# Attention and two feed-forward stages on one core: column norms issued behind the scores, w_out's conversion behind the second normed tile, and the softmax bias from a scaled pass with an accumulator

## The chip, the cores and the metric

The kernel runs on one core of one Trainium2 chip. The metric is the device time of one execution in microseconds (us), lower is better. Five engines work side by side, each through its own queue in order: TensorE (PE, its weight loads PEld), VectorE (DVE), ScalarE (ACT), GpSimd (POOL) and SyncE (SP), which issues the DMAs.

## What is computed

Cut to what matters, with B, H, S, D = 4, 8, 576, 64:

```python
scores = q @ k.T / sqrt(64)
thresh = scores.max(-1) - tau
attn = softmax(where(scores >= thresh, scores, -1e9)) @ v
x = attn as [2304, 512]
xn = x / rms(x) * rms_g
x = (silu(xn @ w_gate) * (xn @ w_val)) @ w_out      # widths 512, 1536
P = Sinkhorn(exp(x @ moe2_w_gate - max), 8 rounds)   # 8 experts
out = sum over e of P[:, e] * (relu(x @ w1[e]) @ w2[e])   # width 1024
```

Large products are made from pairs of f16 numbers (a high and a low part), so every operand is scaled, rounded and split first. The weights of the first feed-forward stage arrive as 64-bit words, from which VectorE and ScalarE build f32 by bit operations.

## The kernel before

The attention runs tile by tile: 144 tiles, a tile being 128 rows of one head (or two heads with 64 rows each). `att_tile` writes the scores S (128 x 576) to one of two PSUM buffers. VectorE takes the row maximum (L292), ScalarE turns it into the bias of the exponential (L293) and into the threshold (L297), and takes the exponential (L296). VectorE zeroes what is below the threshold and sums the rows (L298). ScalarE and GpSimd split the result in two f16 parts (L303 to L305), a DMA transposes it to eT (L307), and `att_values` multiplies it by v (L330). The pv matmuls of a tile are issued three tiles later, behind the scores of that tile (LAG = 3, `tc.issue_after`). `prepare` loads, scales and transposes q, k and v, for the next batch too (ks L225, qs L256, vs L242).

When the eight heads of 128 rows are done, `end_main` and `finish_x` divide by the sums, norm the rows (xn, L353) and transpose them to xnT. Two such tiles are one token group of the first feed-forward stage. `mlp_in` makes 12 blocks gv (L530, 24 matmuls each, both weights) and from each a u (L539, L540) and its parts tT; `mlp_out` multiplies by w_out into two x (L561, 36 matmuls each). There are nine groups. The first can only start when w_gate and w_val are converted (`prep_in`, called six times, by `prep_group`), and its x only when w_out is (`prep_out`).

`prep_in` loads four blocks of words, builds f32 (`to_f32`: L432 on ScalarE; L433, L435 and L436 on VectorE), squares them (L456), and TensorE sums the squares over the partitions into column norms (L457), from which the scale and the two f16 parts follow (L465, L466). The f32 values lie in three stages in the space that later holds w_out. `prep_out` does the like for 12 blocks of w_out with the same `to_f32`, one `words` buffer for the even blocks (x2) and one for the odd (x2t), takes one maximum (womxp, L131), and then scales each block (wof, L507), rounds it (L508) and splits off the rest (L509, GpSimd).

After the attention come the last groups and the second feed-forward stage (h L860, y L906), 16 half experts of dense matmuls.

The program text is not the order: a list scheduler puts each engine's instructions in order by priority at build time, attention first (`attention_order`), and the chip runs each queue as it stands. `tc.issue_after(ins)` puts what a block issues on the engine of `ins` behind `ins` in that engine's queue, and nothing else.

Of the kernel before, what the change touches and what calls it, by code (L numbers as in the profile page):

```python
# [7 lines left out]
F32 = mybir.dt.float32  # L8
F16 = mybir.dt.float16
BF16 = mybir.dt.bfloat16  # L10
I32 = mybir.dt.int32
AF = mybir.ActivationFunctionType
# [7 lines left out]
def kernel(  # L20
# [29 lines left out]
    P = 128  # L50
# [142 lines left out]
    def prep_q_scales(st):  # L193

        b, qr = st["b"], st["raw_q"]
        s_k, i_k = st["k"]
        qm = small([P, NW], "qm", bufs=2)
        for c in range(NW):
            sq = pa.tile([P, H, 2, D], F16, tag="ks", name=f"qq{b}_{c}", bufs=2)
            A.activation(  # L200
                sq[:, :, 0, :].bitcast(BF16), qr[:, :, c, :], AF.Square, accum_out=qm[:, c : c + 1]
            )
        s_q, i_q = norm_scale(qm, NW, 9, f"q{b}")

        wt = small([P, NW], f"wt_{b}")
        bt = small([P, NW], f"bt_{b}")
        V.tensor_scalar(bt, s_q, s_k[:, 0:1], ntau8[:, 0:1], ALU.mult, ALU.mult)
        c2 = small([P, NW], f"c2_{b}")
        V.tensor_scalar(c2, i_q, i_k[:, 0:1], z8[:, 0:1], ALU.mult, ALU.mult)
        V.tensor_scalar(wt, i_q, i_k[:, 0:1], nz8[:, 0:1], ALU.mult, ALU.mult)  # L210
        st.update(wt=wt, bt=bt, c2=c2, s_q=s_q)

    def prep_k(st, a):

# [51 lines left out]
    HS = S // 2  # L266

    waiting = []
    LAG = 3

    def att_tile(st, c, heads, slot, group):

        kT = st["kT"]
        qT, qX = st["q", c]
        nm = f"{st['b']}_{c}_{heads[0]}"
        sums = group["sums"]
        sp = psa.tile([P, 2, 512], F32, tag="S", name=f"S{nm}", bufs=2)
        rows = P // len(heads)
        for qq, first in ((qT, True), (qX, False)):
            for i, h in enumerate(heads):  # L280
                for j in range(2):
                    last = T.matmul(  # L282
                        sp[i * rows : (i + 1) * rows, j, 0:HS],
                        lhsT=qq[:, h, 0:rows],
                        rhs=kT[h // H2][:, h % H2, j * HS : (j + 1) * HS],
                        start=first,
                        stop=not first,
                    )
        sv = sp[:, :, 0:HS]
        nt = pa.tile([P, 3], F32, tag="nt", name=f"nt{nm}", bufs=4)  # L290
        mx = nt[:, 2:3]
        V.tensor_reduce(mx, sv, AX.XY, ALU.max)  # L292
        A.activation(nt[:, 0:1], mx, AF.Copy, scale=st["wt"][:, c : c + 1])  # L293
        e = pa.tile([P, S], F32, tag="e", name=f"e{nm}", bufs=3)
        ev = e.rearrange("p (a n) -> p a n", a=2)
        A.activation(ev, sv, AF.Exp, bias=nt[:, 0:1], scale=st["c2"][:, c : c + 1])  # L296
        A.activation(nt[:, 1:2], mx, AF.Identity, bias=st["bt"][:, c : c + 1])  # L297
        V.scalar_tensor_tensor(  # L298
            ev, sv, nt[:, 1:2], ev, ALU.is_ge, ALU.mult, accum_out=sums[:, slot : slot + 1]
        )  # L300

        hl = pa.tile([P, 2 * S], F16, tag="hl", name=f"hl{nm}", bufs=3)
        A.activation(hl[:, 0:S], e, AF.Copy)  # L303
        G.tensor_tensor(hl[:, S + REM :], e[:, 0 : NCH * P], hl[:, 0 : NCH * P], ALU.subtract)  # L304
        G.tensor_tensor(hl[:, S : S + REM], e[:, NCH * P :], hl[:, NCH * P : S], ALU.subtract)  # L305
        eT = pa.tile([P, 2 * S // P, P], F16, tag="eT", name=f"eT{nm}", bufs=3)
        nc.sync.dma_start_transpose(out=eT, in_=hl)  # L307
        waiting.append((st, heads, slot, group, eT))
        if len(waiting) > LAG:

            with tc.issue_after(last.ins):
                att_values(*waiting.pop(0))
# [25 lines left out]
        return rs  # L338

    xnT = {}  # L340

    def finish_x(i, x, ivx):

        ssq = pa.tile([P, 1], F32, tag="ssq", name=f"ssq{i}", bufs=2)
        xn = pa.tile([P, 2, DM], F16, tag="xn", name=f"xn{i}", bufs=1)
        A.activation(xn[:, 0, :].bitcast(BF16), x, AF.Square, scale=ivx, accum_out=ssq)
        ms = pa.tile([P, 1], F32, tag="ms", name=f"ms{i}", bufs=2)
        V.tensor_scalar(ms, ssq, 1.0 / DM, 1e-6, ALU.mult, ALU.add)
        rs = pa.tile([P, 1], F32, tag="rs", name=f"rs{i}", bufs=2)
        G.tensor_tensor(rs, ms, mhalf, ALU.pow)  # L350
        V.tensor_scalar(rs, rs, 16.0, ivx, ALU.mult, ALU.mult)
        A.activation(xn[:, 0, :], x, AF.Copy, scale=rs[:, 0:1])
        V.scalar_tensor_tensor(xn[:, 1, :], x, rs[:, 0:1], xn[:, 0, :], ALU.mult, ALU.subtract)  # L353
        j, o = i // 2, (i % 2) * P
        if o == 0:
            xnT[j] = pw.tile([P, 2 * KD, 2 * P], F16, tag="xnT", name=f"xnT{j}", bufs=2)
        nc.sync.dma_start_transpose(
            out=xnT[j][:, :, o : o + P], in_=xn.rearrange("p l d -> p (l d)")
        )
# [79 lines left out]
        return lw  # L439

    staged = [0]

    def prep_in(src, w, gi, name):

        bits = src.bitcast(I32)
        raw = stage[:, staged[0] % 3]
        staged[0] += 1
        ps = psm.tile([P, DM], F32, tag="mm", name=f"{name}n{gi}")
        cols = slice(gi * DM, (gi + 1) * DM)
        for kk in range(KD):  # L450
            wd = words(
                bits[kk * P : (kk + 1) * P, 2 * gi * DM : 2 * (gi + 1) * DM], f"{name}w{gi}_{kk}"
            )
            to_f32(raw[:, kk], wd, f"{name}l{gi}_{kk}")
            sq = pw.tile([P, 2 * P], F32, tag="u", name=f"{name}q{gi}_{kk}", bufs=2).bitcast(BF16)
            A.activation(sq, raw[:, kk], AF.Square)  # L456
            T.matmul(ps, lhsT=gsq[:, kk : kk + 1].to_broadcast([P, P]), rhs=sq, start=kk == 0, stop=kk == KD - 1)  # L457
        n2 = small([P, 1], name + "n2", bufs=2)
        V.tensor_reduce(n2, ps, AX.X, ALU.max)
        s, inv = norm_scale(n2, 1, 9, f"{name}{gi}")  # L460
        gs = small([P, KD], f"{name}gs{gi}")
        V.tensor_scalar(gs, g_sb, s[:, 0:1], None, ALU.mult)
        for kk in range(KD):
            sk, hi = gs[:, kk : kk + 1], w[:, 0, kk, cols]
            A.activation(hi, raw[:, kk], AF.Copy, scale=sk)  # L465
            V.scalar_tensor_tensor(w[:, 1, kk, cols], raw[:, kk], sk, hi, ALU.mult, ALU.subtract)  # L466
        return inv
# [14 lines left out]
    def prep_out():  # L482
# [3 lines left out]
        om = small([P, KF], "om")  # L486
        for f in range(KF):
            wd = words(bits[f * P : (f + 1) * P, :], f"wo{f}", ("x2", "x2t")[f % 2])
            sq = to_f32(wo32[:, f], wd, f"wol{f}").bitcast(BF16)[:, 0:DM]
            A.activation(sq, wo32[:, f], AF.Square, accum_out=om[:, f : f + 1])  # L490
        for _ in range(2):
            V.tensor_tensor(
# [488 lines left out]
```

## Time and profile before

| | us |
|---|---|
| median of 3 runs | 2197.92 (2195.69 to 2199.4) |
| profiled execution, its own time | 2195.02 |
| span of that execution, first to last instruction | 2193.2 |
| busy: PE / DVE / ACT / POOL | 2032.0 / 1490.2 / 870.9 / 471.0 |
| chain that ended last | PE 70% of the span |

A busy share is a mean over stages with different limits, so the stages are read one by one, by windows of the trace. A row of waits names who waited, for what, the sum in us, how often and the longest. A row of a group of instructions gives line, engine, operation, output and inputs, shapes, count, busy us, mean ns of one, and the idle time ahead of them with what ended it. Matmuls are pipelined, so the rows of matmuls overlap. Line numbers are those of the kernel before; in the changed kernel the same code stands some 5 to 20 lines further down.

### The profile page before, as it was taken

The numbers are of one execution on the slowest core, as the hardware profiler recorded it, in microseconds if no ns is written. First come the engines' busy times: TensorE is split into PE (matmuls) and PEld (weight loads), VectorE is DVE, ScalarE is ACT, GpSimd is POOL, SyncE is SP. The second block draws the span as 40 slices with busy tenths as digits, with TensorE's granted clock in tenths as the row PEclk, the third lists the DMA queues.
The fourth block names the chain that finished last, engine by engine and source line by source line (L and its number), as shares of the span: only waits on it lengthen the run. The fifth ranks groups of instructions, "written<-read, shape, count | busy, mean of one in ns | idle before, by whom it ended". The sixth has DMA issues, their size and how long they took to land.

```text
span 2193.2 us, 35334 instructions
## 1 busy us (share of the span) xinstructions
PE 2032.0 (93%) x13872; PEld 1194.7 (54%) x13872; DVE 1490.2 (68%) x3026; ACT 870.9 (40%) x1774; POOL 471.0 (21%) x572
## 2 busy tenths in 40 slices
PE   1358789899999999999999999999999999999999
PEld 0236667666876755545555555555555555555554
DVE  6999677777744287865775765766757757666554
ACT  6878778877843243311221221222212212222111
POOL 1347556665743231000000000000000000000000
PEclk9859999999999999999999999999999999999999
DMA  9895879867826051000100100100001001000001
GB/s 267 207 201 100 169 145 174 159 144 115 147 55 142 18 144 40 29 30 1 39 20 20 39 20 20 39 20 20 20 20 39 20 20 39 20 20 1 1 28 60
DMA packets 321879, 154.10 MB, mean 70 GB/s; under 512 B 278960, under 2 KB 292400, under 8 KB 321712
## 3 DMA queue, kind: packets, MB, share of 16 engines
q1 hardware_dynamic: 321120, 151.82, 30.4%
q8 instruction: 108, 1.77, 0.3%
q14 instruction: 59, 0.48, 0.1%
q0 software_dynamic: 64, 0.00, 0.0%
q10 hardware_dynamic: 528, 0.02, 0.0%
HBM read 68.18 MB, written 12.98 MB: 37 GB/s over the span
## 4 chain that ended last, share of the span: by engine, by line
PE 70%; DVE 2%; DMA 1%; SPq 1%; POOL 0%; issue 0%; ACT 0%; DVEq 0%; ACTq 0%
PE y L906 33%; PE h L860 28%; PE gv L530 5%; PE x L561 2%; PE pv L330 1%; DMA w1r<-in_moe_w_dram 1%; SPq L762 0%; PE S L282 0%; DMA x2T<-x2d 0%; DVE w L714 0%; DMA w2r<-in_moe_w_dram 0%; DMA eT<-hl 0%; PE logits L804 0%; DVE w1m L725 0%; POOL xh L601 0%
## 5 line engine op out<-in xcount | busy, mean ns | idle before, releaser
L860 PE MATMUL h<-x2T,w 128*128 128x384 f16 x4032 | 703.8, 326 | 9.9 <-DMA x2T<-x2d 3.9
L860 PEld LDWEIGHTS <-w 128*128 128x128 f16 x4032 | 394.1, 98 | 300.0 <-issue 14.2
L921 DVE SCALAR_TENSOR_TENSOR acc<-y,coef,acc 128x512 f32<-128x512 f32 x270 | 198.1, 746 | 283.0 <-PE y L906 282.9
L730 POOL TENSOR_TENSOR w1s<-w1r 128x512 f32<-128x512 f32 x16 | 20.3, 1271 | 1060.3 <-DMA w1r<-in_moe_w_dram 1006.3
L304 POOL TENSOR_TENSOR hl<-e,hl 128x512 f16<-128x512 f32 x144 | 172.8, 1200 | 228.2 <-ACT hl L303 146.2
L906 PE MATMUL y<-w,hD 128*128 128x512 f16 x864 | 219.9, 379 | 0.0
L906 PE MATMUL y<-w,hA 128*128 128x512 f16 x864 | 210.6, 379 | 0.9 <-DVE acc L921 0.6
L906 PE MATMUL y<-w,hC 128*128 128x512 f16 x864 | 210.0, 379 | 0.2 <-ACT acc L917 0.2
L906 PE MATMUL y<-w,hB 128*128 128x512 f16 x864 | 210.0, 379 | 0.0
L848 ACT ACTIVATE hA<-u 128x384 f16<-128x384 f32 x96 | 50.2, 522 | 341.1 <-DVE u L876 320.9
L848 ACT ACTIVATE hB<-u 128x384 f16<-128x384 f32 x96 | 50.2, 523 | 312.1 <-DVE u L880 311.2
L530 PE MATMUL gv<-xnT,wg 128*128 128x256 f16 x1296 | 167.8, 278 | 4.5 <-DVE u L540 3.0
L530 PE MATMUL gv<-xnT,wv 128*128 128x256 f16 x1296 | 167.5, 275 | 0.0
L330 PE MATMUL pv<-vs,eT 128*128 128x64 f16 (+1 forms) x2240 | 103.1, 201 | 50.3 <-DMA eT<-hl 47.3
L561 PE MATMUL x<-wo,tT 128*128 128x512 f16 x648 | 144.4, 379 | 1.0 <-DVE u L540 0.9
L906 PEld LDWEIGHTS <-hB 128*128 128x128 f16 x864 | 84.5, 98 | 101.9
L530 PEld LDWEIGHTS <-wg 128*128 128x128 f16 x1296 | 126.5, 100 | 24.0 <-issue 4.1
L298 DVE SCALAR_TENSOR_TENSOR e<-S,nt,e 128x576 f32<-128x576 f32 x144 | 116.3, 809 | 32.0 <-ACT e L296 31.5
L906 PEld LDWEIGHTS <-hD 128*128 128x128 f16 x864 | 84.6, 98 | 95.4
L530 PEld LDWEIGHTS <-wv 128*128 128x128 f16 x1296 | 126.4, 99 | 16.0 <-issue 0.2
L906 PEld LDWEIGHTS <-hC 128*128 128x128 f16 x864 | 84.7, 98 | 91.9 <-issue 0.3
L330 PEld LDWEIGHTS <-eT 128*128 128x128 f16 (+1 forms) x2240 | 91.0, 106 | 79.1 <-DMA eT<-hl 62.1
(244 smaller groups left out, 2852.1 us busy)
## 6 DMA issues: line engine op xcount, KB each, us to landing
w1r<-in_moe_w_dram SPq DMA_DIRECT2D x16, 1024.0 KB, 4.9
w2r<-in_moe_w_dram SPq DMA_DIRECT2D x16, 1024.0 KB, 5.3
wgatew<-in_moe_w_gate_dram SPq DMA_DIRECT2D x12, 512.0 KB, 6.0
wo<-in_moe_w_out_dram SPq DMA_DIRECT2D x12, 512.0 KB, 4.2
wvalw<-in_moe_w_val_dram SPq DMA_DIRECT2D x12, 512.0 KB, 4.5
x2d<-xs SPq DMA_DIRECT2D x24, 256.0 KB, 2.5
qX<-qT SPq DMA_DIRECT2D x40, 128.0 KB, 3.5
raw_k<-in_k_dram SPq DMA_DIRECT2D x4, 1024.0 KB, 6.2
```

The source lines that it names most:

```text
L298: V.scalar_tensor_tensor(ev, sv, nt[:, 1:2], ev, ALU.is_ge, ALU.mult, accum_out=sums[:, slot : slot + 1])
L304: G.tensor_tensor(hl[:, S + REM :], e[:, 0 : NCH * P], hl[:, 0 : NCH * P], ALU.subtract)
L330: T.matmul(o, lhsT=a, rhs=r, start=n == 0, stop=n == len(mm) - 1)
L530: T.matmul(gv[:, a, :], lhsT=w[:, l, kk, f * P : (f + 1) * P], rhs=xt[:, r * KD + kk, :], start=n == 0, stop=n == 3 * KD - 1,)
L561: T.matmul(ps, lhsT=tT[f][:, l, o : o + P], rhs=wo[:, f, r, :], start=n == 0, stop=n == 3 * KF - 1,)
L730: G.tensor_tensor(sm[:, 0], a21, a22, ALU.add)
L848: A.activation(t[:, 0, :], src, AF.Relu)
L860: T.matmul(ps, lhsT=w[:, a, l, kk, f * P : (f + 1) * P], rhs=xb[:, b * 4 + r * 2 + kk, :], start=n == 0, stop=n == 5,)
L906: T.matmul(ps, lhsT=hs[a][f][:, l, jj * P : (jj + 1) * P], rhs=w2[:, r, f, :], start=n == 0, stop=n == 3 * KH - 1,)
L921: V.scalar_tensor_tensor(acc[i], ps, coef[h][:, i : i + 1], acc[i], ALU.mult, ALU.add)
```

## The change

It has three parts. In `att_tile` the row maximum and ScalarE's copy are replaced by one VectorE pass that multiplies S by the (negative) scale wt and accumulates the minimum, which is the bias itself; its elementwise output goes to e and is overwritten by the exponential. The threshold is made from the bias by the reciprocal scale w1. In `prep_in` the squares get a buffer of four slots, and the n-th matmul on them is issued behind the scores of tile 3n/4+1. In `prep_out` VectorE's part of `to_f32` is issued behind the second token tile's xn. The per-batch constants move from a buffer each to two shared ones.

```diff
@@ prep_q_scales
-        wt = small([P, NW], f"wt_{b}")
-        bt = small([P, NW], f"bt_{b}")
+        wt = small([P, NW], "wt", bufs=2)
+        bt = small([P, NW], "bt", bufs=2)
         V.tensor_scalar(bt, s_q, s_k[:, 0:1], ntau8[:, 0:1], ALU.mult, ALU.mult)
-        c2 = small([P, NW], f"c2_{b}")
+        c2 = small([P, NW], "c2", bufs=2)
...
+        w1 = small([P, NW], "w1", bufs=2)
+        V.tensor_scalar(w1, i_q, i_k[:, 0:1], -(float(D) ** -0.5), ALU.mult, ALU.mult)
+        V.reciprocal(w1, w1)
@@ att_tile
-        nt = pa.tile([P, 3], F32, tag="nt", name=f"nt{nm}", bufs=4)
-        mx = nt[:, 2:3]
-        V.tensor_reduce(mx, sv, AX.XY, ALU.max)
-        A.activation(nt[:, 0:1], mx, AF.Copy, scale=st["wt"][:, c : c + 1])
+        nt = pa.tile([P, 2], F32, tag="nt", name=f"nt{nm}", bufs=4)
         e = pa.tile([P, S], F32, tag="e", name=f"e{nm}", bufs=3)
         ev = e.rearrange("p (a n) -> p a n", a=2)
+        V.tensor_scalar(
+            ev, sv, st["wt"][:, c : c + 1], None, ALU.mult, ALU.min, accum_out=nt[:, 0:1]
+        )
         A.activation(ev, sv, AF.Exp, bias=nt[:, 0:1], scale=st["c2"][:, c : c + 1])
-        A.activation(nt[:, 1:2], mx, AF.Identity, bias=st["bt"][:, c : c + 1])
+        A.activation(
+            nt[:, 1:2], nt[:, 0:1], AF.Identity, bias=st["bt"][:, c : c + 1],
+            scale=st["w1"][:, c : c + 1],
+        )
...
+        scored.append(last.ins)
@@ finish_x
-        V.scalar_tensor_tensor(xn[:, 1, :], x, rs[:, 0:1], xn[:, 0, :], ALU.mult, ALU.subtract)
+        normed[i] = V.scalar_tensor_tensor(
+            xn[:, 1, :], x, rs[:, 0:1], xn[:, 0, :], ALU.mult, ALU.subtract
+        ).ins
@@ prep_in
+    squares = pw.tile([P, 4, HD], F32, tag="x2t", name="squares")
+    squared = []
...
-            sq = pw.tile([P, 2 * P], F32, tag="u", name=f"{name}q{gi}_{kk}", bufs=2).bitcast(BF16)
+            sq = squares[:, kk, :].bitcast(BF16)
             A.activation(sq, raw[:, kk], AF.Square)
-            T.matmul(ps, lhsT=gsq[:, kk : kk + 1].to_broadcast([P, P]), rhs=sq, start=kk == 0, stop=kk == KD - 1)
+
+            with tc.issue_after(scored[3 * len(squared) // 4 + 1]):
+                T.matmul(ps, lhsT=gsq[:, kk : kk + 1].to_broadcast([P, P]), rhs=sq, start=kk == 0, stop=kk == KD - 1)
+            squared.append(sq)
@@ prep_out
-            sq = to_f32(wo32[:, f], wd, f"wol{f}").bitcast(BF16)[:, 0:DM]
+
+            with tc.issue_after(normed[1]):
+                sq = to_f32(wo32[:, f], wd, f"wol{f}").bitcast(BF16)[:, 0:DM]
```

What this does to the queues shows in two places of VectorE's and one of TensorE's. First VectorE's queue around the second normed tile (xn_850 before, xn_835 in the change); wol is the low word of a block of w_out, and the lines ending in wo on a wo block close its conversion. Before:

```order
L433 TENSOR_SCALAR wol_1663<-wo_1661 128x512
L292 TENSOR_REDUCE nt_2_4_1906<-S_2_4_1901 128x1
L351 TENSOR_SCALAR rs_854<-rs_854,v_i 128x1
L298 SCALAR_TENSOR_TENSOR e_2_3_1876,sums_2_739<-S_2_3_1868,nt_2_3_1873,e_2_3_1876 128x576
L435 SCALAR_TENSOR_TENSOR wol_1663<-wo,wol_1663 128x512
L436 SCALAR_TENSOR_TENSOR wo<-wo_1661,wol_1663 128x512
L433 TENSOR_SCALAR wol_1671<-wo_1669 128x512
L353 SCALAR_TENSOR_TENSOR xn_850<-x_847,rs_854,xn_850 128x512
```

In the change:

```order
L298 TENSOR_SCALAR e_2_4_1867,nt_2_4_1866<-S_2_4_1861,wt 128x576
L483 SCALAR_TENSOR_TENSOR wv<-wo,wvalgs_1177,wv 128x512
L298 TENSOR_SCALAR e_2_5_1906,nt_2_5_1905<-S_2_5_1900,wt 128x576
L483 SCALAR_TENSOR_TENSOR wv<-wo,wvalgs_1177,wv 128x512 x2
L363 SCALAR_TENSOR_TENSOR xn_835<-x_832,rs_839,xn_835 128x512
L445 TENSOR_SCALAR wol_1568<-wo_1566 128x512
L445 TENSOR_SCALAR wol_1576<-wo_1574 128x512
```

Before, nine blocks of w_out have been begun ahead of the second xn; in the change the first follows it.

Then VectorE's queue where w_out's blocks are scaled (wof). Before, between the u of the first group's blocks 5 and 6:

```order
L539 SCALAR_TENSOR_TENSOR u_5_1411<-u_5_1411,gv_5_1386 128x256
L76 TENSOR_SCALAR k_i<-k_i 128x1
L507 TENSOR_SCALAR wof<-wo,wosf 128x512 x2
L540 SCALAR_TENSOR_TENSOR u_5_1411<-u_5_1411,gv_5_1386 128x256
L82 RECIPROCAL k_s<-k_i 128x1
```

In the change, behind all twelve blocks' u:

```order
L520 TENSOR_SCALAR ixs<-wout_i 128x1
L526 TENSOR_SCALAR wof<-wo,wosf 128x512 x2
L83 TENSOR_SCALAR v_s<-v_s 128x1
L84 TENSOR_SCALAR v_i<-v_i 128x1
L229 SCALAR_TENSOR_TENSOR ks_0_0_2140<-raw_k_1892,k_s,ks_0_0_2140 128x4x64 x2
L413 COPY ivr_3198<-v_i 64x1
L229 SCALAR_TENSOR_TENSOR ks_2_0_2147<-raw_k_1892,k_s,ks_2_0_2147 128x4x64 x2
L526 TENSOR_SCALAR wof<-wo,wosf 128x512 x2
L229 SCALAR_TENSOR_TENSOR ks_4_0_2154<-raw_k_1892,k_s,ks_4_0_2154 128x4x64
```

The scaling, and the next batch's ks with it, moved from among the gv blocks to behind the last of them.

Last, TensorE's queue behind the first group's last gv, in the change (x_0 and x_1 are the group's two outputs, womxp the maximum over w_out):

```order
L549 MATMUL gv_11_1534<-xnT_569,wv 128x256
L131 LDWEIGHTS om_1664
L131 MATMUL womxp<-ident,om_1664 128x128
L131 LDWEIGHTS kmm
L131 MATMUL kmxp<-ident,kmm 128x128
L131 LDWEIGHTS vmm
L131 MATMUL vmxp<-ident,vmm 128x128
L580 LDWEIGHTS tT_0_1219
L580 MATMUL x_0_1717<-wo,tT_0_1219 128x512
L580 LDWEIGHTS tT_0_1219
L580 MATMUL x_1_1763<-wo,tT_0_1219 128x512
```

Before, womxp stands behind gv_4 and the first 28 matmuls of x_0 follow each other; in the change x_0 and x_1 alternate in runs of one to three as the blocks of wo become ready.

## Rows read from the trace of the kernel before

**Rows 1.** Windows: stretch, length, busy PE PEld DVE ACT POOL, PEclk, DMA share, GB/s

```profile
19.00:108.00 89.00, 31.31 (x196) 14.91 (x196) 85.84 (x188) 74.21 (x149) 20.64 (x20) 0.93 0.88 237
108.00:152.70 44.70, 20.83 (x183) 12.98 (x182) 41.54 (x91) 35.96 (x78) 19.81 (x22) 0.54 0.88 196
152.70:217.50 64.80, 55.39 (x601) 43.34 (x602) 59.80 (x144) 54.27 (x130) 45.23 (x54) 0.94 0.65 118
217.50:242.70 25.20, 16.50 (x158) 9.34 (x158) 18.11 (x35) 13.60 (x29) 7.56 (x9) 0.92 0.78 167
242.70:610.00 367.30, 342.22 (x3780) 261.16 (x3778) 272.95 (x646) 290.50 (x676) 233.62 (x320) 0.98 0.80 148
...
800.00:2193.00 1393.00, 1380.64 (x7524) 721.69 (x7523) 928.64 (x1724) 332.20 (x573) 76.26 (x58) 1.00 0.08 26
```

**Rows 2.** Timeline around the second xn: start us, us, engine, line, operation

```profile
151.92 0.79 DVE L353 SCALAR_TENSOR_TENSOR xn<-x,rs,xn 128x512 f16<-128x512 f32 x1
152.63 0.74 DVE L292 TENSOR_REDUCE nt<-S 128x1 f32<-128x576 f32 x1
...
156.66 1.68 PE L530 MATMUL gv<-xnT,wg 128*128 128x256 f16 x7 [1.36 <-DMA xnT<-xn]
```

**Rows 3.** VectorE's groups by line, from 108 to 152.7 us

```profile
L298 DVE SCALAR_TENSOR_TENSOR e<-S,nt,e 128x576 f32<-128x576 f32 x10 | 8.0, 803 | 0.0
...
L436 DVE SCALAR_TENSOR_TENSOR wo<-wo,wol 128x512 int32<-128x512 int32 x8 | 6.2, 779 | 0.0
L435 DVE SCALAR_TENSOR_TENSOR wol<-wo,wol 128x512 int32<-128x512 int32 x8 | 5.4, 678 | 0.0
L433 DVE TENSOR_SCALAR wol<-wo 128x512 int32<-128x512 int32 x9 | 4.7, 524 | 3.1 <-DMA wo<-in_moe_w_out_dram 3.1
```

**Rows 4.** The same view, from 242.7 to 610 us

```profile
L298 DVE SCALAR_TENSOR_TENSOR e<-S,nt,e 128x576 f32<-128x576 f32 x105 | 85.0, 811 | 30.3 <-ACT e L296 30.0
```

**Rows 5.** The same view, from 152.7 to 217.5 us

```profile
L507 DVE TENSOR_SCALAR wof<-wo,wosf 128x512 f32<-128x512 f32 x11 | 8.2, 750 | 0.9 <-POOL wo L509 0.9
L225 DVE SCALAR_TENSOR_TENSOR ks<-raw_k,k_s,ks 128x256 f16<-128x256 f32 x5 | 5.0, 1015 | 0.0
...
L256 DVE SCALAR_TENSOR_TENSOR qs<-raw_q,q_s,qs 128x512 f16<-128x512 f32 x1 | 1.4, 1394 | 0.0
...
L82 DVE RECIPROCAL wout_s<-wout_i 128x1 f32<-128x1 f32 x1 | 0.2, 157 | 0.0
```

**Rows 6.** TensorE's timeline, x of the first group

```profile
210.38 6.20 PE L561 MATMUL x<-wo,tT 128*128 128x512 f16 x28
217.52 6.64 PE L561 MATMUL x<-wo,tT 128*128 128x512 f16 x30 [0.94 <-DVE u L540]
```

**Rows 7.** TensorE's timeline, gv of the second group

```profile
242.72 2.72 PE L530 MATMUL gv<-xnT,wg 128*128 128x256 f16 x12
...
248.03 1.47 PE L530 MATMUL gv<-xnT,wg 128*128 128x256 f16 x12
```

**Rows 8.** Line 507: duration ns min/median/max, first and last start us

```profile
L507 DVE TENSOR_SCALAR wof<-wo,wosf x12: 473/532/1365, 186.9 to 221.5; 128x512 f32<-128x512 f32 x12
```

**Rows 9.** Groups by line over the first 900 us

```profile
L292 DVE TENSOR_REDUCE nt<-S 128x1 f32<-128x576 f32 x144 | 107.0, 750 | 32.0 <-PE S L282 31.3
...
L293 ACT ACTIVATE nt<-nt,wt 128x1 f32<-128x1 f32 x144 | 41.3, 287 | 30.1 <-DVE nt L292 29.5
...
L298 DVE DVE_READ_ACCUMULATOR e<-S,nt,e 128x1 f32 x144 | 11.6, 81 | 0.0
...
L433 DVE TENSOR_SCALAR wol<-wo 128x512 int32<-128x512 int32 x12 | 6.0, 498 | 3.9 <-DMA wo<-in_moe_w_out_dram 3.9
```

**Rows 10.** TensorE's waits, 242.7 to 610 us: sum, times, longest

```profile
PE pv L330 <- DMA eT<-hl: 15.9, 18, 2.3
```

**Rows 11.** TensorE's waits, 19 to 108 us

```profile
PE wgaten L457 <- ACT wgateq L456: 24.5, 10, 9.4
...
PE wvaln L457 <- ACT wvalq L456: 8.2, 5, 4.7
```

More of the change, by code (lines that the diff above doesn't have):

```diff
@@ L203, in prep_q_scales @@
         s_q, i_q = norm_scale(qm, NW, 9, f"q{b}")
-        wt = small([P, NW], f"wt_{b}")
-        bt = small([P, NW], f"bt_{b}")
+        wt = small([P, NW], "wt", bufs=2)
+        bt = small([P, NW], "bt", bufs=2)
         V.tensor_scalar(bt, s_q, s_k[:, 0:1], ntau8[:, 0:1], ALU.mult, ALU.mult)
-        c2 = small([P, NW], f"c2_{b}")
+        c2 = small([P, NW], "c2", bufs=2)
         V.tensor_scalar(c2, i_q, i_k[:, 0:1], z8[:, 0:1], ALU.mult, ALU.mult)
         V.tensor_scalar(wt, i_q, i_k[:, 0:1], nz8[:, 0:1], ALU.mult, ALU.mult)
-        st.update(wt=wt, bt=bt, c2=c2, s_q=s_q)
+        w1 = small([P, NW], "w1", bufs=2)
+        V.tensor_scalar(w1, i_q, i_k[:, 0:1], -(float(D) ** -0.5), ALU.mult, ALU.mult)
+        V.reciprocal(w1, w1)
+        st.update(w1=w1, wt=wt, bt=bt, c2=c2, s_q=s_q)
     def prep_k(st, a):
@@ L268 @@
     waiting = []
+    scored = []
     LAG = 3
@@ L340 @@
     xnT = {}
+    normed = {}
     def finish_x(i, x, ivx):
```

## The prediction

> **What bounds the kernel now.** I read the stages first. The windows cut the span at five events: the first block of words at VectorE (19 us), the start of the w_out conversion (108), the second normed tile (152.7), the first token group's last u (217.5), and the second group's first gv (242.7). From 800 us on TensorE is busy 1380.64 of 1393 us, and from 242.7 to 610 still 342.22 of 367.3 [rows 1]. TensorE's work is the same before and after the change, so the time is that work plus what TensorE idles in front of it; a part of the change pays only if the second group's gv comes earlier or if a later wait shrinks. Before 152.7 it is VectorE that is full: 85.84 of 89.0 us, then 41.54 of 44.7, then 59.8 of 64.8 us while the first gv runs [rows 1]. TensorE has 20.83 of 44.7 us there. The first gv starts at 156.66 and waited for the transposed xn, which VectorE had begun at 151.92 [rows 2]. So the front of the kernel is a VectorE queue, and what stands in it before that xn counts.
>
> **Part 1, w_out's conversion behind normed[1].** In the order, nine L433, eight L435 and eight L436 on w_out leave the queue ahead of the second xn. By the rows they take 4.7 + 5.4 + 6.2 = 16.3 us, and VectorE idled 3.1 us for their loads: 19.4 us can go [rows 3]. One wv piece also moves behind, for one more score pass ahead; these cancel. The front will not shrink by all of that, since VectorE is not its only limit: a pv for tile t-3 stands on TensorE between two tiles' scores, so four tiles share one pass through scores, exp, threshold, split and transpose. Ten tiles pass in these 44.7 us, 4.5 us each; where VectorE has room, 105 tiles pass in 367.3 us, 3.5 us each [rows 1, 3, 4]. At that pace ten tiles need 35.0 us. I take **-9.7 us** for the first gv; the ends are 0 (something else sets that pace) and -19.4.
>
> What moved has to be done before x of the first group, as x reads wo. The gv stage now gets the 16.3 us and, by the order, loses 11 wof scalings (8.2 us), five ks (5.0), one qs (1.4) and some 25 small ops on [128,1] or [128,5] at about 0.157 us (3.9): 18.5 us out [rows 5]. With a wv piece, an xn and slightly longer score passes in, that nets to **0**; the ends are the 5.0 us that VectorE idles there, either way. On SyncE ten of eleven loads that stay behind the first are now issued between eT transposes, each once its words buffer is free, so a transpose behind one can be held for a conversion of some 2 us (0.52 + 0.68 + 0.78) [rows 3]. TensorE is busy 55.39 of 64.8 us there [rows 1] and has gv for cover; without it, each such hold is a late pv.
>
> The 18.5 us that left come back between the last gv and the second group. There the order has womxp behind gv_11, then the scales, then 12 wof with ks among them, and x_0 and x_1 in small pieces that follow each wo block. Before, x ran as 28 matmuls from 210.38 and 30 from 217.52, with wo long there [rows 6], and the second group began at 242.72 [rows 7]. VectorE idled 7.1 of those 25.2 us [rows 1]. At the means the stage grows by 18.5 - 7.1 = 11.4 us. I take less: the median wof is 0.53 us, not 0.75, (2.4 us off) [rows 5, 8], and about 42 instructions start some 0.08 us before the one ahead ends, as the L292 at 152.63 does behind the xn that ends at 152.71 (3.4 us off) [rows 2]: **+5.6 us**. Ends: 0, if ACT's and TensorE's waits there are filled, and +11.4.
>
> **Part 2, the bias from the scaled pass.** L292 (750 ns) becomes a TENSOR_SCALAR over the same S with an accumulator; ACT loses the L293 copy (287 ns) [rows 9]. No row has that form. From below: a TENSOR_SCALAR of 512 from SBUF at 498 ns, 0.56 us for 576; from above: the L298 pass at 811 ns [rows 4] with its accumulator read of 81 ns, 0.89 us. I take 0.75 + 0.08 = 0.83 us, since it streams the same S from PSUM as L292. VectorE pays 0.08 us a tile: 22 tiles in the front make 1.8 us, hidden if the tile pace binds there and paid if VectorE does (ends -4 and +3 us); from 242.7 on VectorE has 94 us of room. The tile's chain loses 0.29 and gains 0.08: 0.2 us. TensorE waits for eT 18 times in that stage, 15.9 us in all [rows 10]; 18 x 0.2 = **-3.7 us**. Ends: 0 and -15.9. ACT's 41.3 us less are off the path.
> For the lower end of the pass, the Trainium skill (VectorE: DVE Perf Modes, "Why PSUM operands drop a tier") says that a PSUM operand in fp32 keeps VectorE at one element a cycle; by it 0.56 us is out of reach and the -4 us above falls away, while the sum stays.
>
> **Part 3, column norms behind scores.** TensorE waits 24.5 and 8.2 us for squares between 19 and 108 [rows 11], but VectorE is free for 3.2 of those 89 us [rows 1], so scores that come sooner find it taken. I cost this at nothing. If the cover went (ACT stuck on a square whose buffer waits for a norm behind a late score), a tile's pace of 3.5 us is lost each time. The four squares also hold the buffer of w_out's odd words, so those can load only after the last norm, behind tile 18's scores.
>
> **Sum**: -9.7 + 0 + 5.6 - 3.7 = -7.8 us. The profiled execution took 2195.0 us (span 2193.2), so 2187.2; the runs' median is 2.9 us above it: **2190.1 us**. About 0.2% (4.4 us) is what a measurement can tell from no change.
>
> **Rivals.**
> *Given back (same).* VectorE's work up to 242.7 is only re-ordered: 19.4 us leave and return. It idled 18.4 us in the four stages; if that stays, nothing is won there, the passes of the 39 tiles before it (144 less 105) add 39 x 0.08 = 3.1 us, and -3.7 remains: about 2197.3. For it: the density above. Against: 3.1 of the idle is the wait for w_out's loads, 7.1 is in the stage that the work moves into.
> *The x stage gets exposed (slower).* Its x matmuls now follow wof, ACT and POOL block by block. Where TensorE was sparse its granted clock was 0.54, between the two levels (20.83 of 44.7 us busy); at 55.39 of 64.8 it was 0.94 [rows 1]. 28 x took 6.20 us [rows 6], so 72 take 15.9. Twelve gv of the second group took 2.72 us from 242.72 and 1.47 us from 248.03 [rows 7], as at the lower level, 1.2 GHz, and at 2.4 GHz: 1.85 times as long. So x takes 29.4 us, the stage grows by 5.6 + 13.5 = 19.1, the sum is +5.7 and the time 2203.6. It decides once that stage grows by more than 13.4 us. Against it: 16.5 of 25.2 us busy kept 0.92 [rows 1].
> The Trainium skill (TensorE: Matmul & The Clock Gate, "HAM oscillation — how this bites in real kernels") says that waits between short bursts of matmuls bring the clock down each time; by that rule this rival holds, where the 0.92 above speaks against it.
> *The front is VectorE's alone (faster).* All 19.4 us go: 9.7 more, about 2180.
> *The change does not do what it says* for the norms: scores move up on TensorE but no result moves; that is already in the sum.
>
> **Numbers.** My forecast 0.45, given back 0.23, exposed 0.20, front alone 0.12. The range takes in the first, second and fourth with some of the unknown ends (3 us below the fourth), and the exposed case to some 2 us past its point: 2177 to 2206. Within my forecast the ends of its terms put about a fifth above -4.4 us, mostly into no change. So: faster 0.53, same 0.25, slower 0.22.
>
> **What would show it.** Right: first gv near 147, VectorE's wait for w_out gone from the front, second group's gv near 238, the score pass near 0.83 us with a read of about 0.08, waits for eT below 15.9 us after it. Wrong: the first gv past 152 (the tile pace or ACT's squares bind earlier), the stage between last gv and second group above 38 us or at a clock well below 0.9, or a score pass near 1 us. If the first gv is early and the second group is not, the gain was given back.

## The result, and the profile after

The change makes the kernel slower: 2221.12 us median against 2198.66, a ratio of 1.0103 (95% interval 1.0088 to 1.0118), some 22.5 us. The prediction was 2190.1 us, and its range ended at 2206. The profiled execution of the changed kernel took 2221.37 us; that of the kernel before (2195.02) lay 3.6 us under its median, so differences between the two profiles come out near 26 us.

The windows of the changed kernel, cut at its own events: first gv (149.0), first x (216.3), first gv of the second group (260.9), and then the same lengths as before [rows 1]. Columns as there.

```profile
19.00:108.00 89.00, 31.45 (x214) 17.33 (x215) 80.82 (x193) 74.17 (x142) 24.41 (x25) 0.80 0.95 237
108.00:149.00 41.00, 19.23 (x182) 12.26 (x183) 37.96 (x93) 27.97 (x49) 15.95 (x18) 0.58 0.71 150
149.00:216.30 67.30, 49.93 (x560) 40.49 (x558) 60.58 (x157) 51.03 (x113) 35.87 (x46) 0.93 0.80 165
216.30:260.90 44.60, 28.14 (x210) 13.38 (x210) 32.85 (x69) 27.53 (x54) 19.35 (x19) 0.81 0.58 121
260.90:628.20 367.30, 333.08 (x3733) 257.63 (x3731) 275.83 (x741) 280.42 (x565) 232.93 (x320) 0.97 0.79 145
826.30:2219.00 1392.70, 1380.57 (x7524) 721.58 (x7521) 928.80 (x1724) 331.39 (x573) 75.97 (x58) 1.00 0.08 26
```

The last row is the old one, 26 us later: nothing is lost there. The loss lies ahead. TensorE's timeline of the changed kernel from its first gv to the first h shows where it grows (start, us, operation; in brackets the idle time ahead and what ended it):

```profile
149.04 2.11 PE L549 MATMUL gv<-xnT,wg 128*128 128x256 f16 x9
...
208.81 0.60 PE L549 MATMUL gv<-xnT,wv 128*128 128x256 f16 x4
210.23 0.23 PE L131 MATMUL womxp<-ident,om 128*128 128x128 bf16 x1 [0.82 <-DVE om L518]
211.86 0.22 PE L131 MATMUL kmxp<-ident,kmm 128*128 128x128 bf16 x1 [1.40 <-DVE womx L133]
212.46 0.22 PE L131 MATMUL vmxp<-ident,vmm 128*128 128x128 bf16 x1 [0.38 <-DVE kmx L133]
216.32 1.01 PE L580 MATMUL x<-wo,tT 128*128 128x512 f16 x2 [3.65 <-ACT wo L527]
...
224.60 2.85 PE L580 MATMUL x<-wo,tT 128*128 128x512 f16 x12 [0.64 <-POOL wo L528]
236.13 0.66 PE L287 MATMUL S<-kT,qT 128*128 128x288 f16 x4
...
241.28 1.04 PE L580 MATMUL x<-wo,tT 128*128 128x512 f16 x4
...
260.87 2.75 PE L549 MATMUL gv<-xnT,wg 128*128 128x256 f16 x12
...
706.18 1.14 PE L879 MATMUL h<-x2T,w 128*128 128x384 f16 x6 [3.88 <-DMA x2T<-x2d]
```

The same events on TensorE of the kernel before:

```profile
178.12 0.22 PE L131 MATMUL womxp<-ident,om 128*128 128x128 bf16 x1
...
183.49 0.22 PE L131 MATMUL kmxp<-ident,kmm 128*128 128x128 bf16 x1
...
207.90 1.47 PE L530 MATMUL gv<-xnT,wv 128*128 128x256 f16 x12
...
223.99 0.65 PE L282 MATMUL S<-kT,qT 128*128 128x288 f16 x4
...
228.17 1.69 PE L561 MATMUL x<-wo,tT 128*128 128x512 f16 x7
...
678.99 1.44 PE L860 MATMUL h<-x2T,w 128*128 128x384 f16 x4 [3.89 <-DMA x2T<-x2d]
```

Read against [rows 2, 6, 7], four steps make 27.2 us up to the first h; 0.9 us of them is gone again at the end:

| event | before | after | lost since the event above | the prediction's term |
|---|---|---|---|---|
| first gv | 156.7 | 149.0 | -7.7 | -9.7 |
| first group's last gv ends | 209.4 | 209.4 | +7.7 | 0 |
| second group's first gv | 242.7 | 260.9 | +18.2 | +5.6 |
| first h | 679.0 | 706.2 | +9.0 | -3.7 |

The gv came early as forecast, and the lead was gone at the end of the first group's gv. TensorE's waits (sum, times, longest) in that stage, before (156.66 to 209.37) and after (149.04 to 209.41), show where:

```profile
PE pv L330 <- DMA eT<-hl: 3.0, 2, 2.1
...
PE gv L530 <- DVE u L540: 0.5, 2, 0.3
```

```profile
PE pv L339 <- DMA eT<-hl: 6.5, 5, 2.5
PE gv L549 <- DVE u L559: 4.2, 5, 1.2
```

And the engines' busy time in the same two stretches, columns as in the windows above:

```profile
156.66:209.37 52.71, 47.14 (x543) 39.35 (x544) 48.87 (x117) 43.19 (x106) 37.02 (x45) 0.97 0.68 123
```

```profile
149.04:209.41 60.37, 49.23 (x556) 40.15 (x553) 53.78 (x126) 47.48 (x104) 32.18 (x41) 0.95 0.82 170
```

Then w_out's maximum stands behind the last gv, at 210.23 where it was at 178.12, and with it the maximum of the next batch's K (211.86, was 183.49). VectorE's timeline of the changed kernel shows what hangs on them:

```profile
211.53 0.28 DVE L133 TENSOR_REDUCE womx<-womxp 128x1 f32<-128x128 f32 x1
212.12 0.28 DVE L133 TENSOR_REDUCE kmx<-kmxp 128x1 f32<-128x128 f32 x1
...
214.11 0.87 DVE L526 TENSOR_SCALAR wof<-wo,wosf 128x512 f32<-128x512 f32 x2
215.02 0.87 DVE L229 SCALAR_TENSOR_TENSOR ks<-raw_k,k_s,ks 128x256 f16<-128x256 f32 x2
```

Scaling of w_out starts at 214.11 where it started at 186.92, and scaling of the next batch's k at 215.02 where it was 191.86:

```profile
186.92 1.23 DVE L507 TENSOR_SCALAR wof<-wo,wosf 128x512 f32<-128x512 f32 x2
...
191.86 1.30 DVE L225 SCALAR_TENSOR_TENSOR ks<-raw_k,k_s,ks 128x256 f16<-128x256 f32 x1
```

So from 210 to 236 TensorE has first a gap and then x in pieces, with waits of 0.3 to 0.9 us between them for the next block of wo, and no scores at all. The second batch's first scores (those of tile 36, counting from 0) come at 236.13 instead of 223.99.

The new pass and its neighbours, groups over the first 900 us, against [rows 9]:

```profile
L298 DVE TENSOR_SCALAR_CACHE_REDUCE e<-S,wt 128x576 f32<-128x576 f32 x144 | 115.7, 811 | 22.8 <-PE S L287 15.9 <-POOL hl L313 4.9 <-PE pv L339 0.7
...
L298 DVE DVE_READ_ACCUMULATOR e<-S,wt 128x1 f32 x144 | 11.8, 82 | 0.0
```

```profile
L302 ACT ACTIVATE nt<-nt,bt,w 128x1 f32<-128x1 f32 x144 | 54.3, 377 | 0.0
```

The pass is 0.81 + 0.08 = 0.89 us where I took 0.83, and the threshold, which now also multiplies, takes 377 ns; before, `L297` took 281:

```profile
L297 ACT ACTIVATE nt<-nt,bt 128x1 f32<-128x1 f32 x144 | 40.5, 281 | 0.0
```

The chain from scores to threshold is then 0.29 us shorter by the copy and longer by 0.14 for the pass and 0.10 for the threshold: about 0.05 us gained, not 0.2. TensorE's waits for eT grew instead of shrinking [rows 10]; over 260.9 to 628.2 us:

```profile
PE pv L339 <- DMA eT<-hl: 28.1, 20, 4.0
```

How the 9.0 us behind 260.9 come about shows when both kernels are cut at 600 us and the work of one line is counted: thresholds with their accumulator reads (two instructions a tile) on VectorE, then gv and x on TensorE. The columns are busy us with the count, for TensorE the weight loads too, then clock, DMA share and GB/s. Before:

```profile
0.00:600.00 600.00, 114.16 (x280) 0.93 0.81 166
0.00:600.00 600.00, 212.12 (x1728) 168.30 (x1728) 0.93 0.81 166
0.00:600.00 600.00, 83.92 (x373) 35.37 (x374) 0.93 0.81 166
```

After:

```profile
0.00:600.00 600.00, 112.37 (x274) 0.90 0.81 164
0.00:600.00 600.00, 191.68 (x1543) 151.09 (x1544) 0.90 0.81 164
0.00:600.00 600.00, 83.90 (x360) 34.54 (x360) 0.90 0.81 164
```

The score tiles are 3 behind (140 and 137), but gv is 185 matmuls behind: at 0.109 us each (12 in 1.31 us, the step between two rows of gv at the higher clock) 20.2 us, with 13 x at 0.22 us 2.9 more. That work is done when attention is over. Counting tiles from 0, the threshold of tile 40 starts at 253.4 before and 259.5 after, that of tile 140 at 602.6 and 608.7: both kernels take 349.2 us for these 100 tiles, the changed one with less gv beside them (1305 against 1368). The tiles are a conveyor with a pace of 3.49 us, and what gv does not get done beside them is added at the end.

### The profile page after: what moved, and what is told of

Same layout as the page of the kernel before. It is cut to its first block, busy times and chain, and to the rows that moved or that the text cites. A ratio compares the mean times of both kernels' runs of the same rounds, so it can differ in the third digit from the quotient of the medians.

```text
span 2219.5 us, 35391 instructions
## 1 busy us (share of the span) xinstructions
PE 2034.8 (92%) x13871; PEld 1197.2 (54%) x13872; DVE 1501.6 (68%) x3178; ACT 860.2 (39%) x1630; POOL 470.3 (21%) x572
## 4 chain that ended last, share of the span: by engine, by line
PE 72%; DVE 8%; DMA 7%; ACT 4%; issue 4%; POOL 3%; SPq 2%; ACTq 0%; DVEq 0%; POOLq 0%
PE y L925 33%; PE h L879 28%; PE gv L549 6%; PE x L580 3%; DMA eT<-hl 3%; DVE e L298 1%; DMA kT<-ks 1%; POOL hl L312 1%; ACT e L301 1%; PE pv L339 1%; DVE e L306 1%; PE S L287 1%; DMA qT<-qs 1%; ACT hl L311 1%; DVE wo L448 1%
## 6 DMA issues: line engine op xcount, KB each, us to landing
x2d<-xs SPq DMA_DIRECT2D x24, 256.0 KB, 2.4
```

## The experiments

In each table row, time is the median and the ratio is that to the kernel before on the same chip. "tile 40" and "tile 140" are the start of that tile's threshold pass, "gv2" the second group's first gv, in the profiled execution.

| run | us | ratio (95% interval) | first gv | gv2 | tile 40 | tile 140 |
|---|---|---|---|---|---|---|
| before | 2198.66 | | 156.7 | 242.7 | 253.4 | 602.6 |
| after | 2221.12 | 1.0103 (1.0088 to 1.0118) | 149.0 | 260.9 | 259.5 | 608.7 |
| only_pass | 2219.04 | 1.0097 (1.0083 to 1.011) | 154.5 | 248.6 | 259.1 | 619.6 |
| only_norms | 2211.47 | 1.0056 (1.0041 to 1.007) | 148.2 | 241.7 | 260.3 | 617.8 |
| only_wout | 2214.47 | 1.0073 (1.006 to 1.0086) | 149.1 | 253.2 | 263.6 | 611.8 |
| norms_wout | 2210.71 | 1.0062 (1.0049 to 1.0075) | 146.0 | 243.5 | 254.0 | 605.6 |
| pass_old_order | 2205.97 | 1.0028 (1.0018 to 1.0038) | 158.9 | 245.5 | 256.3 | 607.8 |
| max_new_order | 2214.65 | 1.0068 (1.0049 to 1.0087) | 152.6 | 244.6 | 257.2 | 613.8 |
| after_old_late | 2213.67 | 1.0063 (1.0046 to 1.008) | 148.8 | 257.4 | 267.7 | 616.6 |
| norms_old_late | 2208.91 | 1.0039 (1.0025 to 1.0054) | 148.5 | 242.5 | 266.0 | 615.3 |
| max_after_order | 2222.97 | 1.0109 (1.0095 to 1.0123) | 148.2 | 257.7 | 256.0 | 607.3 |
| tables_alone | 2210.95 | 1.0051 (1.0039 to 1.0064) | 161.3 | 243.7 | 255.2 | 622.7 |
| wout_old_late | 2206.61 | 1.0029 (1.0019 to 1.0039) | 147.3 | 254.5 | 264.6 | 612.2 |
| holds_old_late | 2207.79 | 1.0035 (1.0022 to 1.0047) | 148.3 | 247.7 | 262.9 | 614.9 |
| after_own_psum | 2222.09 | 1.0103 (1.009 to 1.0116) | 149.7 | 280.0 | 238.3 | 605.0 |
| own_psum_old_late | 2210.94 | 1.0058 (1.0045 to 1.007) | 151.0 | 259.3 | 268.4 | 624.2 |
| before_own_psum | 2220.81 | 1.01 (1.0087 to 1.0113) | 164.4 | 273.9 | 237.2 | 602.7 |
| holds_own_psum_late | 2205.82 | 1.0027 (1.0016 to 1.0039) | 150.8 | 256.8 | 264.8 | 612.7 |

### One part of the change at a time

Each of the first four runs takes the diff's hunks of one part (or of both holds, a hold being an `issue_after`) and leaves the other lines as before.

only_pass: the tables of `prep_q_scales` and the new lines of `att_tile`.

```diff
-        V.tensor_reduce(mx, sv, AX.XY, ALU.max)
-        A.activation(nt[:, 0:1], mx, AF.Copy, scale=st["wt"][:, c : c + 1])
...
+            ev, sv, st["wt"][:, c : c + 1], None, ALU.mult, ALU.min, accum_out=nt[:, 0:1]
```

> The kernel before with the scaled pass alone (bias from VectorE's accumulator; norms and w_out's conversion as before). Theory A (the two losses add up, and the pass holds the one after the x stage): the chain scores to threshold is not shorter, since the pass with its read is 0.89 us where it was 0.75 and the threshold on ScalarE 0.38 where it was 0.28; VectorE pays 0.14 us a tile, so some 5 us on the front and 8 to 9 us from the second group on: 2203 to 2213 us, and the stage between the last gv of the first group and the first gv of the second stays within 5 us of before. Rival B (the pass is what I forecast, and the loss after the x stage comes from the work that w_out's hold pushed there): 2191 to 2199 us. Rival C (no part loses by itself, only the order made from all three does): within 4 us of before.

only_norms: `squares`, `scored`, `squared` and the `issue_after` in `prep_in`.

```diff
+            sq = squares[:, kk, :].bitcast(BF16)
...
+            with tc.issue_after(scored[3 * len(squared) // 4 + 1]):
```

> The kernel before with the norms' hold and their squares buffer alone. Theory A: within 4.4 us of before (2194 to 2203), first gv of the first group 0 to 3 us earlier. Rival B says the same. Rival C (norms behind scores delay the conversions, and w_out's odd words wait for the last norm): first gv later than 158 us and a time over 2203.

only_wout: `normed` and the `issue_after` in `prep_out`.

```diff
+            with tc.issue_after(normed[1]):
                 sq = to_f32(wo32[:, f], wd, f"wol{f}").bitcast(BF16)[:, 0:DM]
```

> The kernel before with w_out's hold alone. Theory A (x of the first group is exposed behind the scaling of w_out): first gv of the first group near 148 to 150 us, first gv of the second group 8 to 18 us later than the 242.7 of before, and this is kept to the end: 2207 to 2216 us. Rival B (the hold costs that and what lies after it): 2215 to 2225. Rival C (the hold alone is harmless; it is the held norms, whose squares hold the buffer of w_out's odd words, that make it late): 2188 to 2199.

norms_wout: both of these diffs.

> The changed kernel without the scaled pass: the maximum and ScalarE's copy are back, both holds stay. Theory A: the second group's first gv 13 to 19 us later than before, and no more lost after it: 2208 to 2216 us. Rival B: as the changed kernel or worse, 2219 to 2228. Rival C (the three only lose together): within 4.4 us of before.

Measured: +20.7, +13.1, +16.1 and +12.4 us against the 2198.33 of these runs. Each part alone loses, and both holds together no more than either. No theory expected all of that. Theory A has the times of only_wout and norms_wout in its bands, but in norms_wout by a gv2 13 to 19 us late, and it was 0.8 us late; A and B held the norms' hold for free, and only_pass lost 6 us more than A's band. Rival C held the pass and w_out's hold for free, and where it expected a loss, in only_norms, it was by a late first gv, which came 8.5 us early. Nor do parts add up to the 22.5 us of the whole. What all four share is that the list scheduler put the whole program in a new order, far from the lines that were edited: only_norms has its gv2 1.0 us early and still loses.

### Instructions and order apart

To tell the two apart I pinned an order: the position of every instruction in each engine's queue is taken from one kernel and imposed on another by ordering edges that carry no wait.

```diff
+    for key, text in ORDER.items():
+        row = array.array("h", zlib.decompress(base64.b85decode(text)))
+        row = [i for i in (LOG[key].log[j] for j in row) if i is not None]
+        for p, n in zip(row, row[1:]):
+            tc.add_manual_dep(n, p.name, mybir.DependencyInfo(mybir.DependencyClass.NoSync, mybir.DependencyReason.DATA), reason="order")
```

pass_old_order has the instructions of the pass and the order of the kernel before; max_new_order the old instructions and the order of only_pass.

> The scaled pass's instructions, but every engine in the order of the kernel before (the planner's order is pinned to it, tile by tile). Theory O (the instructions cost little, and the 20.7 us of the pass alone come from the order that the planner made anew for the whole program): 2196 to 2204 us, the second group's gv within 3 us of 242.7. Rival P (the pass, the read and the slower threshold themselves lengthen each tile): 2212 to 2222 us.

> The other half of the cross: the instructions of the kernel before (maximum, ScalarE's copy), but every engine in the order that the planner made for the scaled pass alone. Theory O: 2211 to 2221 us, as with the pass. Rival P: 2195 to 2203 us, as before.

2205.97 and 2214.65 us: from 2199.41, the instructions cost 6.6 us in the old order, and the order alone costs 15.2 with the old instructions; together 21.8, where only_pass lost 20.7. Theory O holds for most of it, with 2 us more for the instructions than it gave. In pass_old_order gv2 is 2.8 us late, in the stages where VectorE is full (38 tiles by 0.14 us are 5.4 at most), and tile 140 is 5.2 us late, so nearly half is paid behind, where VectorE has room. The traces show that the order did go over: by the tile that each matmul writes, TensorE's queue in pass_old_order is that of the kernel before, and in max_new_order that of only_pass. No run pins a kernel to its own order, so what the pinning itself costs is not known; whatever it is in the first of these runs, it lies within the 6.6 us.

max_after_order is the same for the whole change: the instructions of the kernel before, in the changed kernel's order.

> The instructions of the kernel before (maximum, ScalarE's copy; the squares buffer of the change), every engine in the order of the changed kernel. Theory O (the order costs most, the pass some 6 us as in the cross on the pass alone): 2212 to 2219 us, first gv of the second group 254 to 260. Rival P (the pass's instructions carry the loss, and the order was made for them): 2198 to 2208 us.

2222.97 us: as slow as the changed kernel, and slower than theory O said. Rival P falls. In this order the pass costs nothing that can be measured; the order, holds and all, takes the whole loss. TensorE's timeline of this run shows the same place with the old maximum and copy in it:

```profile
208.50 0.23 PE L143 MATMUL womxp<-ident,om 128*128 128x128 bf16 x1 [1.85 <-DVE om L523]
210.13 0.22 PE L143 MATMUL kmxp<-ident,kmm 128*128 128x128 bf16 x1 [1.40 <-DVE womx L145]
...
257.69 0.61 PE L554 MATMUL gv<-xnT,wg 128*128 128x256 f16 x2
...
704.94 0.48 PE L884 MATMUL h<-x2T,w 128*128 128x384 f16 x1 [4.29 <-DMA x2T<-x2d]
```

tables_alone asks how little is enough. It is the kernel before with the four small tables in shared buffers and w1 computed, which nothing reads:

```diff
-        wt = small([P, NW], f"wt_{b}")
+        wt = small([P, NW], "wt", bufs=2)
...
+        w1 = small([P, NW], "w1", bufs=2)
+        V.tensor_scalar(w1, i_q, i_k[:, 0:1], -(float(D) ** -0.5), ALU.mult, ALU.mult)
+        V.reciprocal(w1, w1)
```

> The kernel before with only the four small per-batch tables of the change (two more operations of [128,5] a batch, shared buffers), used by nothing; the planner orders anew. Theory O: those 8 operations take under 2 us themselves, but the order of the whole program is dealt anew, womxp stands later and the time is 2204 to 2222 us. Rival N (an order made anew for no reason is as good as the old one): 2196 to 2203 us.

2210.95 us, +10.7, from eight operations of [128,5] and four tables in shared buffers. The two were not taken apart, but pass_old_order has both as well, and with the old order it lost 6.6 us with the pass in it. That the order is another shows in the trace: 1378 gv stand ahead of the scores of tile 100 on TensorE where 1315 stood. Its gv2 is 1.0 us late, its first h, at 694.74, is 15.75 us late. Rival N falls: the order of the kernel before is better by some 10 us than what the scheduler deals for nearly the same program.

### The lag made in front, and what comes behind

In the next four runs only the late part of the old order is pinned: TensorE from the second group's first gv on, the other engines from tile 38 on. The edit is the one above, with tables that begin there; what comes earlier stands as the scheduler puts it for the changed kernel, the norms' hold, w_out's hold, and both holds.

> The changed kernel with the order of the kernel before pinned from the second group's first gv on (TensorE) and from the 39th score tile on (the other engines); what comes earlier stands as the planner puts it for the change. Theory O: the 18 us by which that gv is late stay, the 8.6 us lost behind it go: 2210 to 2217 us. Rival P (they are the pass's own): 2218 to 2226 us.

> The norms' hold alone, with the order of the kernel before pinned from the second group on in the same way. Alone it had that gv 1 us early and was 13 us late by the first h. Theory O: 2193 to 2201 us. Rival P (something that the hold and its squares buffer leave behind costs time later): 2206 to 2214 us.

> w_out's hold alone with the old order from the 39th tile on. Alone, with its own order, it had the second group's gv 10.5 us late, tile 36 10 us late, and 2214.5 us. Theory L (with the old order behind it, the score tiles keep the lag that they have at tile 40, no more and no less): lag 8 to 14 us at tile 40 and 2207 to 2213 us. Rival M (the lag is made up behind, where TensorE has gv to do): 2198 to 2206 us.

> Both holds without the scaled pass, old order from the 39th tile on. With its own order it had the first gv 10.7 us early, tile 36 3.4 and tile 40 0.6 us late, and 2210.7 us. Theory L: 2197 to 2204 us. Rival M: 2188 to 2196 us, since the early first gv pays.

after_old_late: 2213.67 us, as theory O said. Of the changed kernel's loss of 22.5 us, 8.2 go with the old late order and 14.3 stay. Its gv2 is 14.7 us late, its first h (692.86) 13.9. The split is not wholly one of front and rear: the old order has 24 gv of the second group ahead of the scores of tile 40, the changed kernel none, so the pin made tile 40 8.2 us later than it was (267.7 for 259.5).

norms_old_late was expected at 2193 to 2201 and took 2208.91: a miss. gv2 was on time, but tile 40 was 12.6 us late, and tile 140 was 12.7 late. I had taken gv2 for the mark; the tiles are. The other three runs of this group show the same: 14.3 us late at tile 40 and 14.0 at tile 140 (after_old_late), 11.2 and 9.6 (wout_old_late), 9.5 and 12.3 (holds_old_late). So theory L is right in kind and rival M falls, by the tiles (by its time alone wout_old_late lies between the two): with the old order the lag of the tiles is carried to the end, within some 3 us. (One run of the next group, own_psum_old_late, goes from 15.0 to 21.6 us late; its profiled execution had a span of 2216.3 us, over its median of 2210.94.) wout_old_late came out 0.4 us under its band, holds_old_late 3.8 us over, since pinning made its tile 40 later than its own order had (254.0). Part of a lag of that kind may come from where the two orders meet.

### The small buffer

w_out's maximum and those of K and V share one small PSUM buffer in the order of the text, so K's cannot run ahead of w_out's. In three runs w_out's goes into a wide buffer:

```diff
+        if name == "womx":
+            ps = psm.tile([P, DM], F32, tag="mm", name=name + "p")[:, 0:P]
+        else:
             ps = psm.tile([P, P], F32, tag="mx", name=name + "p", bufs=1)
```

> The changed kernel, with w_out's maximum in one of the wide PSUM buffers instead of the one small buffer that the maxima of K and V use in turn; the planner orders anew. Theory Q (w_out's late maximum holds that buffer, so the next batch's K maximum, its k scaling, its transposes and its first scores come late, and the score tiles carry this lag to the end): kmxp runs before 190 us instead of 211.9, the first score of the second batch starts before 229 instead of 236.1, and the time is 2203 to 2215 us, some of the planner's new order still in it. Rival X (x of the first group, paced by w_out's scaling, sets the second group alone): the second group's gv stays at 257 to 262 and the time at 2218 to 2224 us.

> The same with the order of the kernel before pinned from the 39th tile on, as in the run of the changed kernel that took 2213.7 us. Theory Q: the lag of tile 40 (14.3 us there) falls below 7 and the time to 2199 to 2208 us. Rival X: 2211 to 2217 us.

> Both holds, no scaled pass, w_out's maximum in a wide PSUM buffer, the order of the kernel before from the 39th tile on. Both holds alone had the first gv 10.7 us early and tile 36 3.4 us late. Theory Q: tile 40 is 0 to 8 us earlier than before and the time 2190 to 2199 us, the first version with a gain. Rival X: the second group's gv stays within 2 us of 243.5 and tile 40 late, 2199 to 2206 us.

> The kernel before with w_out's maximum in a wide PSUM buffer and nothing else; the planner orders anew and puts that maximum behind the last gv of the first group, K's far ahead. Theory Q: K's maximum was held by little in the kernel before (178 to 183.5 us), so what shows is mostly the new order and w_out's later scaling, 2195 to 2213 us. Rival X (x paced by w_out's scaling sets the second group): that gv 8 to 18 us later, 2206 to 2216 us.

In after_own_psum the maximum of the second batch's K runs at 91.38 us instead of 211.86, its first scores at 217.94 instead of 236.13, and tile 40 starts at 238.3 instead of 259.5. So the buffer did hold them, the first half of theory Q. But the time is 2222.09 us, and there the theory fails: x now starts at 235.42 and gv2 at 279.95. The two wide buffers are taken in the order of the text too, so w_out's maximum has to follow the last gv; and here the step over its twelve blocks that the maximum needs ran on VectorE only at 220.3 us, where it ran at 210.0 in the changed kernel.

```profile
217.94 0.64 PE L290 MATMUL S<-kT,qT 128*128 128x288 f16 x2 [0.69 <-DVE e L309]
...
221.84 0.29 PE L134 MATMUL womxp<-ident,om 128*128 128x128 bf16 x1
...
235.42 1.04 PE L583 MATMUL x<-wo,tT 128*128 128x512 f16 x2
...
279.95 1.25 PE L552 MATMUL gv<-xnT,wg 128*128 128x256 f16 x5
```

before_own_psum loses as much (2220.81) with x at 231 us; there that step ran at 182.4, and womxp came at 218.67, behind the last gv. Tiles ahead by 16 us at tile 40 do not help when TensorE has no gv to run beside them: at tile 140 before_own_psum is level with the kernel before (602.7 and 602.6), but has 1554 gv done against 1728. The other two, with the old late order, took 2210.94 (Theory Q said 2199 to 2208) and 2205.82 (2190 to 2199): both slower than expected. The old late order has no use for early tiles: tile 36 is 10.8 and 17.3 us early, but tile 40 has to follow the first 24 gv of the second group, and these come at 259.3 and 256.8. No version that beats the kernel before came out of these runs.

## Why the prediction was wrong

**The front: right in place, near in size.** -9.7 was forecast for the first gv, -7.7 measured; VectorE's wait for w_out left the front as described. only_wout alone has -7.6, only_norms -8.5 and both together -10.7: either hold gives most of it. So part 3, costed at nothing, was not nothing there: in only_norms 9 of the 25 instructions of w_out's conversion are left ahead of the second xn, without any hold on them.

**"That nets to 0" (the gv stage) failed.** The stage took 60.4 us where it took 52.7, and the ends of 5.0 us did not hold 7.7. The sums of VectorE's time were out by 0.8 to 4.9 us: it is busy 60.58 us where it was 59.80 in the windows above, whose ends differ, and 53.78 where it was 48.87 from the first gv to the end of the last. VectorE's wait for w_out's loads, 3.1 us in front before, is here now:

```profile
L445 DVE TENSOR_SCALAR wol<-wo 128x512 int32<-128x512 int32 x10 | 4.2, 422 | 3.8 <-DMA wo<-in_moe_w_out_dram 3.8
```

On TensorE 3.7 us more went into gv waiting for u, on a VectorE that had the conversions in its queue, and 3.5 more into pv waiting for eT, the late pv that the prediction named and did not price. Which of VectorE, ScalarE and SyncE made each eT late was not looked into.

**The x stage failed, by the rival that was named and for another reason.** I priced what VectorE has to do there (18.5 us less 7.1 of idle) and not the chain that has to come first: last block of w_out, maximum, scales, first scaled block, first x. The maximum starts 32 us later (178.12 to 210.23) and takes K's maximum with it, through the shared buffer. 18.2 us were lost, above the term's upper end of 11.4 and near the 19.1 of the exposed rival. They fall into three: the first x comes 6.9 us behind the last gv where it was 1.0; x takes 26.0 us from its first to its last where it took 19.5; and the second group's gv follows 18.6 us behind x where it was 12.9, with the scores of four tiles between them where those of two stood. The whole from the last gv to the second group's is 51.5 us, over the 38 that the prediction had named as a sign of being wrong. The rival gave 13.5 of its 19.1 us to the clock, and there it was right for the start of x alone. Twelve x took 2.85 us in the middle of the stage, near the 2.65 that 28 in 6.20 make [rows 6], and the granted clock was 0.96 from 217.5 to 242.7:

```profile
209.40:216.30 6.90, 0.68 (x4) 0.31 (x4) 6.77 (x32) 3.56 (x10) 3.67 (x6) 0.74 0.65 124
216.30:219.50 3.20, 2.86 (x7) 0.95 (x7) 3.20 (x4) 0.77 (x2) 2.55 (x2) 0.50 0.45 91
217.50:242.70 25.20, 20.52 (x134) 8.99 (x133) 17.25 (x32) 13.08 (x30) 13.27 (x12) 0.96 0.32 62
242.70:260.90 18.20, 6.61 (x74) 4.14 (x75) 14.40 (x36) 13.96 (x25) 4.92 (x7) 0.61 0.95 203
```

It fell to the lower level (0.50, 1.2 GHz) in the gap ahead of x, where TensorE was busy 0.68 of 6.9 us, and the first seven x ran at it: 2.86 us, where an estimate from 28 in 6.20 gives seven 1.55. It fell again behind x, to a mean of 0.61, where TensorE was busy 6.61 of 18.2 us. The Trainium skill (TensorE: Matmul & The Clock Gate, "HAM oscillation — how this bites in real kernels") describes bursts of matmuls with longer waits between them, each of which brings the clock down, a condition that the prediction left out. The gap ahead of x agrees; the waits of 0.3 to 0.9 us between x's bursts are shorter than most of these bursts, so the 0.96 is no test of it.

**The pass was mis-sized, and its -3.7 had the wrong sign.** 0.89 us for 0.83, and 0.10 us for the slower threshold left out. Worked through, the chain gains 0.05 us a tile, not 0.2. Instead of less than 15.9 us TensorE waits 28.1 for eT from gv2 on. In the old order the instructions cost 6.6 us.

**The steps that failed, by size.** Against the prediction's terms the steady stage is off by 12.7 us (-3.7 forecast, +9.0 measured), the x stage by 12.6, the gv stage by 7.7 and the front by 2.0. The x and gv stages are terms that were written down, with the new order read, and priced by VectorE's busy time where the chain of waits decides. Behind them stands a step that was not written as a term: that outside the parts named, the order stays. The steady stage was costed on the old order, 18 waits by 0.2 us. The runs show that the order costs: 2222.97 us with the old instructions in the new order, and 10.7 us from eight tiny operations and shared buffers, with no hold. I had read the new order at the places of the terms, and had not counted it where I had no term.

In the changed kernel's TensorE queue gv stands later relative to the score tiles through most of the attention: 336 ahead of tile 44's scores where 408 stood, 1572 ahead of tile 140's where 1728 stood. That could be counted without a time. But it is no sure mark of a worse order: in only_norms and tables_alone gv stands earlier (1344 and 1378 ahead of tile 100's scores where 1315 stood), and both lose, by tiles that are 15 and 20 us late at tile 140.

What stays open: which edit of the order in front would let w_out's hold keep its 7.7 us. The own-buffer runs moved the loss from the tiles to x and did not tell whether an earlier maximum alone would do; that was not tried. Why the scheduler's new order is worse was not looked into either.

## What to carry to other kernels

Where a scheduler orders the program, an edit has two prices, that of its instructions and that of the new order, and the second can be the larger: measure them apart by pinning the old order under the new instructions, and the new under the old. When work is moved behind something, follow the last piece of it to all who wait, through the small buffers that its result shares with others. And in a pipeline of tiles with filler work (here the score tiles, with gv beside them), count both at a late point: a tile lag is carried to the end, and so is filler that was not there to fill.

## What was not expected of the hardware

VectorE's scaled pass with an accumulator took 811 ns on 128x576 from PSUM plus an 82 ns read, as long as the pass of two inputs with an accumulator (811 and 81 [rows 4, 9]), and 61 ns more than the plain maximum (750). On ScalarE an operation on [128,1] took 377 ns with a tensor for scale and for bias, 281 with a tensor for the bias alone: one more operand cost 96 ns.
